# Attention masks placed in PSUM by ScalarE, a sum of squares taken on TensorE, and a new listed order

## The chip, the core and the metric

The kernel runs on one core of a Trainium2 chip. A core has a matrix engine (TensorE, PE in the profile; its weight loads are shown apart as PEld), a vector engine (VectorE, DVE), a scalar engine (ScalarE, ACT), GpSimd (POOL), and SyncE (SP), which here only issues DMAs. Each engine works through its own instructions in the order in which they are written, and waits on semaphores where another engine or a DMA has to be done first. On-chip data lies in SBUF, and the matrix products land in PSUM, which has 8 banks of 512 floats for each of 128 partitions.

The metric is the device time of one launch in microseconds (us). The kernel before was timed three times: 518.71, 516.87 and 521.91 us, median 518.71. The execution whose profile is read below took 516.67 us.

## What is computed

Batched attention with two kinds of masks, then a feed-forward layer with the SoLU activation (h times softmax of h), a layer norm and a second product. Cut to what matters:

```python
# B, H, S, D = 8, 8, 576, 64; d_model 512, d_ff 1024
rel = pos[:, None] - pos[None, :]
mask_local = (rel >= 0) & (rel < 32)                    # heads 0 to 3
mask_strided = (rel >= 0) & (pos_k % 32 == pos_q % 32)  # heads 4 to 7
scores = where(mask, q @ k.T / sqrt(D), -1e9)
x = softmax(scores) @ v              # laid out as 4608 tokens x 512
h = x @ w_in
solu = h * softmax(h)
ln = (solu - mean(solu)) / sqrt(var(solu) + 1e-6) * g_ln
out = ln @ w_out
```

w_in and w_out come as 64-bit floats, and the kernel decodes them on the chip.

## The kernel before

**Tiling.** For each of 8 batches the attention is cut into 5 units, 40 in all; `unit(n)` works on batch n // 5. Units 0 and 1 of a batch are strided (6 and 5 blocks of 54 queries by 54 keys, for two pairs of heads), units 2 to 4 are local (3 blocks of 64 queries by 96 keys). The feed-forward part runs over 36 tiles of 128 tokens, `ff(n)`. A tile can start when the units that write its tokens are done.

**A unit.** `qk` (the step that ends at line 364) fills the two PSUM banks of `s_ps` with the scores of the unit: first four products of a 64x64 unit matrix with the bf16 mask (line 359) write 0 or -8e9 over the banks and open the accumulation, then the products of queries and keys (line 364, four 64x64 quarters of the array side by side) add to them. There is one `s_ps`, so the next unit's `qk` can start only when VectorE has taken the row maximum (L370) and subtracted it into SBUF (L380); for the few units of `BY_BLOCK` ScalarE reads the banks instead (L375). Then come exponentials (L382), row sums (L383), a reciprocal (L387, L388), the scaling on GpSimd (L391), a split into two f16 parts (ScalarE L397, VectorE L398), a transposing DMA into one of two `pt` buffers (SP, L400), the products with the values (`pv`, L421) into `x_ps`, and the split of the result into `xhi` and `xlo` (L439, L440). `pv` of a local unit reads the values partly through a shifted copy `ve`, that of a strided unit through `vd`; SP fills both by DMA from the split values (L335).

**A feed-forward tile.** `g1` does two halves of 12 products into `h_ps` (L482 to L484); maxima, exponentials and sums follow on VectorE and ScalarE (L488 to L498), the norms on GpSimd (L502 to L537), the split into `cc` (L544, L545), a transposing DMA (L548), then two halves of 12 products with w_out (`g2`, L557 to L559) and the store (L565, L566).

**Weights.** `prep_w` loads w_in in four chunks of 1 MB, decodes each (ScalarE L585, VectorE L588 and L589), squares each on ScalarE with a running sum (L598) and has TensorE add the sums over the partitions (L260). A power of two near the root, `w_sc`, then scales the chunks into two f16 parts (L603, L604). `prep_o` does the like for w_out, in four chunks of 1 MB, and folds the mean and the gain into it with eight products (L624). `v_scale(b)` finds such a scale for the values of batch b (ScalarE L299, TensorE L260, VectorE L266 to L272), and takes one column of `s_ps` for its sum; `v_split` splits the values (L320, L321).

**What sets the order.** The steps are recorded with `plan.add(engine, assumed duration, function, reads, writes)`, and then issued in the order of a table of step numbers, `ORDER`, which was found by a search outside the kernel. Each engine, and SP's queue of DMAs, runs its part of that list in order; semaphores guard the data.

Of the kernel before, what the change touches and what calls it, by code (L numbers as in the profile page):

```python
# [20 lines left out]
P = 128  # L21
# [21 lines left out]
SQ = 20  # L43

# [5 lines left out]
EARLY = 4  # L50
BY_BLOCK = (2, 3, 4, 7, 8, 9)
# [22 lines left out]
833 730 857 1074 729 889 704 622 726 890 732 625 731 626-628 613 733 630 734 891 631 705 905 614 737 706 632 878 845 879 735 880 750 906 615 907 835  # L74
# [16 lines left out]
1293 1294 1186-1188 1171 1428 1189 1155 1266 1297 1267 1295 1172 1385 1296 1173 1287 1156 1429 1312 1288 1420 1191 1421 1410 1192 1310 1430 1193 1298  # L91
# [6 lines left out]
1472 1518 1519 1510 1520 1522 1521 1511 1473 1523-1526 1540 1527 1474 1533 1529 1542 1541 1531 1534 1530 1532 1492 1543 1535 1536 1544 1545 1547 1546  # L98
1548 1493 1549-1552 1537 1494 1553 1554 1508 1528 1558 1555 1556 1559 1557 1538 1560 1561 1512 1539 1513 1562 1514 1563 1564
"""  # L100


class Plan:
    def __init__(self):
        self.steps = []
        self.issue = {}
        self.writer, self.readers = {}, {}

# [34 lines left out]
def attn_solu_kernel(ctx: ExitStack, tc: tile.TileContext, qloc, qstr, kloc, kstr, vloc, vstr, w_in, w_out, g, masks, out):  # L143
# [7 lines left out]
    def buf(name, shape, dtype=F32, n=1):  # L151
        return [sb.tile(shape, dtype, name=f"{name}{i}") for i in range(n)]
# [589 lines left out]
```

## Time and profile before

| what | value |
|---|---|
| three timed runs | 518.71, 516.87, 521.91 us |
| the profiled execution | 516.67 us, of which 515.0 us from the first to the last instruction |
| mean granted TensorE clock | 0.983 |
| HBM read, written | 39.24 MB, 9.44 MB |
| `pt` and `cc` transposing DMAs | 40 and 42 issues, median 4.6 and 4.4 us from issue to landing |
| w_in chunks | 4 of 1024 KB, median 14.1 us to landing |

The page gives busy time by engine, the span in 40 slices of 12.9 us, the chain of work that ended last, and the groups of instructions by line, with the mean duration of one and the idle time of the engine before them. A matmul's recorded duration includes the time in the pipeline: successive matmuls start well before the one before has ended, so the cost of a matmul on a full TensorE is read from start to start.

### The profile page before, as it was taken

To read this page: it belongs to the slowest core of one execution; us is meant where nothing else is said; L and a number is where in the kernel's file an instruction comes from. 1 tells how busy PE (TensorE), PEld (TensorE's weight loads), DVE (VectorE), ACT (ScalarE), POOL (GpSimd) and SP (SyncE) were. 2 spreads that over 40 slices of the span, in tenths; PEclk is the share of its full clock that TensorE was granted. 3 is DMA by queue.
4 is the path that set the end of the run, shared out by engine and by line. 5 is a ranking of instruction groups with operands and counts; after the bars stand their busy time and mean duration, and the time that the engine had idled before them with its cause. 6 is when DMAs were issued, how large, how long until landed. Compare 5 with 4: busy or idle time off the path is not lost.

```text
span 515.0 us, 11938 instructions
## 1 busy us (share of the span) xinstructions
PE 469.2 (91%) x4780; PEld 240.6 (47%) x4780; DVE 361.3 (70%) x745; ACT 314.2 (61%) x586; POOL 173.4 (34%) x350
## 2 busy tenths in 40 slices
PE   2223799999999999999999999999999999999997
PEld 2123444445455545454555454544554444444443
DVE  2968898869787777787787757866795577554430
ACT  3897577686755676737665666555564656355541
POOL 5211012635244433323343325035524225115330
PEclk9997599999999999999999999999999999999999
DMA  8999997659879999987999996665996287633542
GB/s 330 376 270 276 297 262 184 189 149 190 171 160 254 207 235 294 234 193 150 216 211 211 246 185 155 103 127 138 233 221 124 62 147 149 134 76 78 123 87 77
DMA packets 155351, 96.90 MB, mean 188 GB/s; under 512 B 138272, under 2 KB 138912, under 8 KB 154784
## 3 DMA queue, kind: packets, MB, share of 16 engines
q1 hardware_dynamic: 150112, 86.71, 76.2%
q10 hardware_dynamic: 5184, 9.44, 5.3%
q8 instruction: 37, 0.61, 0.5%
q14 instruction: 18, 0.15, 0.1%
HBM read 39.24 MB, written 9.44 MB: 95 GB/s over the span
## 4 chain that ended last, share of the span: by engine, by line
PE 79%; DMA 8%; ACT 4%; DVE 4%; SPq 2%; POOL 1%; issue 1%; ACTq 0%; DVEq 0%; POOLq 0%
PE h_ps L482 11%; PE o_ps L557 11%; PE h_ps L484 10%; PE h_ps L483 10%; PE o_ps L559 10%; PE o_ps L558 10%; PE x_ps L421 5%; PE s_ps L364 5%; DMA pt<-p 5%; DMA k<-kloc 2%; PE o_ps L624 2%; PE s_ps L359 1%; DMA vrs<-vstr 1%; ACT raw L492 1%; DVE obuf L640 1%
## 5 line engine op out<-in xcount | busy, mean ns | idle before, releaser
L482 PE MATMUL h_ps<-w,xhi 128*128 128x512 f16 x280 | 106.4, 380 | 1.1 <-DVE raw L494 0.9
L484 PE MATMUL h_ps<-w,xlo 128*128 128x512 f16 x280 | 106.1, 379 | 0.0
L483 PE MATMUL h_ps<-w,xhi 128*128 128x512 f16 x280 | 106.1, 379 | 0.0
L557 PE MATMUL o_ps<-obuf,cc 128*128 128x512 f16 x272 | 103.4, 380 | 0.9 <-issue 0.9
L559 PE MATMUL o_ps<-obuf,cc 128*128 128x512 f16 x272 | 103.1, 379 | 0.0
L558 PE MATMUL o_ps<-obuf,cc 128*128 128x512 f16 x272 | 103.1, 379 | 0.0
L391 POOL TENSOR_TENSOR t<-t,m 128x576 f32<-128x576 f32 (+2 forms) x40 | 48.6, 1218 | 117.6 <-DVE m L388 100.2
L488 DVE TENSOR_REDUCE st<-h_ps 128x1 f32<-128x512 f32 x70 | 46.9, 684 | 53.0 <-PE h_ps L484 52.8
L492 ACT ACTIVATE raw<-h_ps,st,vsc 128x512 f32<-128x512 f32 x62 | 47.9, 775 | 32.0 <-DVE st L490 30.7
L525 POOL TENSOR_SCALAR st<-st 128x1 f32<-128x1 f32 x32 | 12.8, 399 | 152.9 <-DVE st L497 144.3
L498 ACT ACTIVATE raw<-raw,st 128x1024 f32<-128x1024 f32 x36 | 41.3, 1146 | 27.7 <-DVE st L497 21.7
L545 DVE SCALAR_TENSOR_TENSOR cc<-raw,st,cc 128x1024 f16<-128x1024 f32 (+1 forms) x38 | 48.3, 1275 | 12.6 <-ACT cc L544 12.4
L544 ACT ACTIVATE cc<-raw,st 128x1024 f16<-128x1024 f32 (+1 forms) x38 | 41.6, 1100 | 24.8 <-POOL st L534 24.2
L494 DVE SCALAR_TENSOR_TENSOR raw<-h_ps,raw 128x512 f32<-128x512 f32 x70 | 47.4, 682 | 10.3 <-ACT raw L492 9.7
L565 ACT ACTIVATE ob<-o_ps,st 128x512 f32<-128x512 f32 x34 | 23.4, 687 | 48.3 <-PE o_ps L559 38.8
L364 PE MATMUL s_ps<-k,q 64*54 64x54 f32 (+1 forms) x1280 | 41.9, 275 | 4.3 <-DMA k<-kloc 2.6
L370 DVE TENSOR_REDUCE m<-s_ps 128x6 f32<-128x576 f32 (+2 forms) x40 | 30.4, 760 | 21.6 <-PE s_ps L364 21.5
L484 PEld LDWEIGHTS <-xlo 128*128 128x128 f16 x288 | 28.2, 98 | 34.4 <-DVE xlo L440 0.5
L559 PEld LDWEIGHTS <-cc 128*128 128x128 f16 x288 | 28.2, 98 | 34.0
L482 PEld LDWEIGHTS <-xhi 128*128 128x128 f16 x288 | 28.1, 98 | 33.2 <-issue 1.3
L557 PEld LDWEIGHTS <-cc 128*128 128x128 f16 x288 | 28.1, 98 | 33.0 <-issue 1.1
L483 PEld LDWEIGHTS <-xhi 128*128 128x128 f16 x288 | 28.2, 98 | 31.7 <-issue 1.8
(134 smaller groups left out, 760.7 us busy)
## 6 DMA issues: line engine op xcount, KB each, us to landing
out<-ob ACTq DMA_DIRECT2D x36, 256.0 KB, 3.6
vd<-vs SPq DMA_DIRECT2D x16, 384.0 KB, 6.4
q<-qstr SPq DMA_DIRECT2D x8, 594.0 KB, 6.1
k<-kstr SPq DMA_DIRECT2D x8, 594.0 KB, 5.9
q<-qloc SPq DMA_DIRECT2D x8, 576.0 KB, 5.1
k<-kloc SPq DMA_DIRECT2D x8, 576.0 KB, 6.3
raw<-w_in SPq DMA_DIRECT2D x4, 1024.0 KB, 14.1
vrs<-vstr SPq DMA_DIRECT2D x5, 768.0 KB, 7.4
```

Source lines behind the costliest of these rows:

```text
L364: nc.tensor.matmul(s_ps[row : row + nq, pair, i * nk : (i + 1) * nk], q_raw[half][hs, q0 : q0 + (nq - 1) * nqb + 1 : nqb], k_raw[half][hs, ...
L391: add("pool", nx * nk / 520 + 0.03, lambda: nc.gpsimd.tensor_tensor(tv, tv, sm.unsqueeze(2).broadcast_to([P, nx, nk]), op=ALU.mult), r=TM, ...
L482: nc.tensor.matmul(hv[i], xhi[:, cc, tok], whi[:, cc, cols], start=(cc == 0), stop=False)
L483: nc.tensor.matmul(hv[i], xhi[:, cc, tok], wlo[:, cc, cols], start=False, stop=False)
L484: nc.tensor.matmul(hv[i], xlo[:, cc, tok], whi[:, cc, cols], start=False, stop=(cc == 3))
L488: add("dve", 0.69, lambda i=i: nc.vector.tensor_reduce((nm, nm2)[i], hv[i], axis=AX.X, op=ALU.max, negate=True), r=[HH[i]], w=[(ST, "nm", i)])
L492: add("act", 0.73, lambda i=i, q=q: nc.scalar.activation(e[:, parts2[i]], hv[i], AF.Exp, bias=nm, scale=hs, accum_out=q), r=[HH[i], (ST, " ...
L494: add("dve", 0.7, lambda i=i, x=x: nc.vector.scalar_tensor_tensor(u[:, parts2[i]], hv[i], 1.0, e[:, parts2[i]], op0=ALU.mult, op1=ALU.mult ...
L545: add("dve", w / 980 + 0.23, lambda cols=cols: nc.vector.scalar_tensor_tensor(c[:, 1, cols], u[:, cols], r, c[:, 0, cols], op0=ALU.mult, o ...
L557: nc.tensor.matmul(o, ct[:, cc, :], ohi[:, cc, :], start=(cc == 0), stop=False)
L558: nc.tensor.matmul(o, ct[:, cc, :], olo[:, cc, :], start=False, stop=False)
L559: nc.tensor.matmul(o, ct[:, 8 + cc, :], ohi[:, cc, :], start=False, stop=(cc == 7))
```

## The change

Three edits.

1. From unit 6 on (`SEEDED = NU + 1`) the four mask products are gone. A new step on ScalarE, `seed`, copies the bf16 mask into both banks of `s_ps` (f32), once for each unit, and the query-key products add to what it wrote. The step reads the masks and writes `s_ps`, so it waits for the last reader of the unit before, and `qk` waits for it. The assumed duration of `qk` falls by 0.2 us. The column that `v_scale` uses in `s_ps` moves with the batch, and its product no longer opens an accumulation from batch 2 on.
2. In `prep_w` the four squares on ScalarE (L598) are gone. After each chunk's decode, TensorE multiplies the chunk (the upper 16 bits of each float, read as bf16) with itself, in 8 products of 128x128 that all add up in one bank, and after the fourth chunk VectorE takes the diagonal with a running sum (`diag`). The decode scales by a further power of two.
3. `ORDER` is a new table.

```diff
+W_SHIFT = 24
+SEEDED = NU + 1
 ORDER = """
-1 5 8 10 4 11 16 13 12 29 14 9 6 56 155 44 2 57 58 0 71 59 7 15 45 17 60 21 25 72 30 46 61 73 62 47 48 3 50 31 91 74 86 75 76 63 92 77 93 94 87 64 116
+7 3 0 4 8 10 11 16 13 15 12 14 9 29 6 17 25 57 156 21 45 5 58 59 2 1 72 60 61 46 62 73 63 47 74 48 92 75 49 76 51 77 93 78 30 94 52 87 18 31 53 64 95
...
     def pow2_scale(...):
-                nc.tensor.matmul(tot, ones, part.bitcast(BF16)[:, 1:2], start=(i == 0), stop=(i == len(parts) - 1))
+                nc.tensor.matmul(tot, ones, part.bitcast(BF16)[:, 1:2], start=(i == 0 and not adds), stop=(i == len(parts) - 1), skip_group_check=adds)
...
     def v_scale(b):
-        room = (s_ps[:, 1, 511:512], ("s", 1)) if b else (h_ps[2][:, 0:1], ("h", 2))
+        room = (s_ps[:, 1, 512 - b : 513 - b], ("s", 1)) if b else (h_ps[2][:, 0:1], ("h", 2))
...
     def unit(n):
+        mk = (mk_loc[:, 0 if b0 == 0 else 1] if half == 0 else mk_str[:, 0:nb]).rearrange("p x k -> p (x k)")
+        if n >= SEEDED:
+            def seed():
+                nc.scalar.copy(s_ps[:, :, 0 : nb * nk], mk.unsqueeze(1).broadcast_to([P, 2, nb * nk]))
+            add("act", nx * nk / 1200 + 0.17, seed, r=["mask"], w=[("s", 0), ("s", 1)])
         def qk():
-            for pair, h, hs, row in heads:
+            for pair, h, hs, row in heads if n < SEEDED else ():
                 nc.tensor.matmul(s_ps[row : row + D, pair, 0 : nb * nk], unit_sb[hs, hs], mk[hs], start=True, stop=False)
...
-        add("pe", nb * 0.231 + (0.25, 0.09)[half], qk, ...)
+        add("pe", nb * 0.231 + (0.25, 0.09)[half] - (0.2 if n >= SEEDED else 0.0), qk, ...)
...
     def prep_w():
         for cc in range(4):
-            add("act", 1.15, lambda cc=cc: nc.scalar.activation(ob_sb[cc % 2].bitcast(BF16), stage[cc], AF.Square, scale=2.0**-SQ,
-                                                                accum_out=w_sc[:, 4 + cc : 5 + cc]),
-                r=ST[cc], w=[("wm", cc), ("ob", cc % 2)])
-        pow2_scale(w_sc, [w_sc[:, 4 + cc : 5 + cc] for cc in range(4)], ..., (h_ps[0][:, 0:1], ("h", 0)))
+            def gram(cc=cc):
+                x = stage[cc].bitcast(BF16).rearrange("p (f t) -> p f t", t=2)[:, :, 1]
+                for i in range(8):
+                    nc.tensor.matmul(h_ps[0][:, 0:P], x[:, i * P : i * P + P], x[:, i * P : i * P + P], start=(cc == 0 and i == 0), stop=(cc == 3 and i == 7))
+            add("pe", 0.6, gram, r=ST[cc], w=[("h", 0)])
+        add("dve", 0.3, lambda: nc.vector.scalar_tensor_tensor(diag, h_ps[0][:, 0:P], 1.0, unit_sb, op0=ALU.mult, op1=ALU.mult, accum_out=w_sc[:, 4:5]),
+            r=[("h", 0), "unit"], w=["wm"])
+        pow2_scale(w_sc, [w_sc[:, 4:5]], ["wm"], "w_sc", (h_ps[1][:, 0:1], ("h", 1)), mul=2.0**W_SHIFT, shift=0, floor=2.0**-64)
```

Line numbers in the rows of the changed kernel are its own: L411 is the transposing DMA of a unit (L400 before), L339 the copies of values (L335), L285 the loads (L281), L362 the new mask copy, L408 and L450 what L397 and L439 were.

**SP's queue, batch 0, from the transposing DMA of unit 1 to that of unit 2.** `pt1<-p1`, `pt1<-p0` and `pt0<-p2` are the transposing DMAs of units 1, 3 and 2, `ve` the shifted copy of the local values in three pieces, `raw<-w_out` chunks of w_out. Before:

```order
L400 DMA_TRANSPOSE pt1_98<-p1_95 128x10x128
L281 DMA q00_63<-qloc 128x1152
L281 DMA raw0_67<-w_out 128x2x1024
L400 DMA_TRANSPOSE pt1_98<-p0_94 128x12x128
L335 DMA ve0_73<-vl0_71 64x2560
L335 DMA ve0_73<-vl0_71 32x2x1024
L335 DMA ve0_73<-vl0_71 32x2x256
L281 DMA raw0_67<-w_out 128x2x1024
L400 DMA_TRANSPOSE pt0_97<-p2_96 128x12x128
L281 DMA cc0_101<-w_out 128x2x1024
```

Now:

```order
L411 DMA_TRANSPOSE pt1_98<-p1_95 128x10x128
L285 DMA raw0_67<-w_out 128x2x1024
L285 DMA q00_63<-qloc 128x1152
L411 DMA_TRANSPOSE pt1_98<-p0_94 128x12x128
L339 DMA ve0_73<-vl0_71 64x2560
L411 DMA_TRANSPOSE pt0_97<-p2_96 128x12x128
L285 DMA raw0_67<-w_out 128x2x1024
L339 DMA ve0_73<-vl0_71 32x2x1024
L339 DMA ve0_73<-vl0_71 32x2x256
L285 DMA cc0_101<-w_out 128x2x1024
```

Unit 2's transposing DMA moved ahead of the second w_out chunk, and two of the three pieces of `ve` moved behind that chunk.

**ScalarE, batch 0, around the squares of w_in.** `p` rows are the f16 split of a unit, `t,m<-s_ps` its exponentials, `junk,vm1` the squares of the values of batch 1. Before:

```order
L397 CAST p2_96<-t2_87 128x6x96
L299 ACTIVATE junk0_68,vm1_76<-vrs0_70 128x1536
L598 ACTIVATE ob0_102,w_sc0_114<-cc0_101 128x1024
L598 ACTIVATE ob1_103,w_sc0_114<-cc0_101 128x1024
L598 ACTIVATE ob0_102,w_sc0_114<-cc0_101 128x1024
L598 ACTIVATE ob1_103,w_sc0_114<-cc0_101 128x1024
L397 CAST p0_94<-t3_88 128x6x96
L375 ACTIVATE t0_85,m4_93<-s_ps_118,m4_93 128x96 x6
L439 CAST xhi0_99<-x1_ps_123 128x18x18
```

Now:

```order
L303 ACTIVATE junk0_68,vm1_76<-vrs0_70 128x1536
L408 CAST p2_96<-t2_87 128x6x96
L408 CAST p0_94<-t3_88 128x6x96
L386 ACTIVATE t0_85,m4_93<-s_ps_119,m4_93 128x96 x6
L450 CAST xhi0_99<-x1_ps_124 128x18x18
L450 CAST xhi0_99<-x0_ps_123 128x18x18
```

The four squares are gone, and the splits of units 2 and 3 stand next to each other.

**ScalarE, batches 2 and 3, around units 15 and 16.** `raw,st<-h_ps` rows (L492, now L503) are exponentials of feed-forward tiles, `raw<-raw` (L498, now L509) their squares, `cc<-raw` (L544, now L555) their splits, `t<-t` (L382, now L393) the exponentials of a unit. Before:

```order
L439 CAST xhi0_99<-x1_ps_123 128x18x18
L439 CAST xhi0_99<-x0_ps_122 128x18x18
L382 ACTIVATE t2_87<-t2_87 128x576
L397 CAST p0_94<-t0_85 128x6x96
L492 ACTIVATE raw0_67,st3_107<-h2_ps_121,st3_107,vsc1_78 128x512
L492 ACTIVATE raw0_67,st3_107<-h0_ps_119,st3_107,vsc1_78 128x512
```

Now:

```order
L393 ACTIVATE t2_87<-t2_87 128x576
L450 CAST xhi0_99<-x0_ps_123 128x18x18
L362 CAST s_ps_119<-mk_str0_83 128x2x324
L450 CAST xhi0_99<-x1_ps_124 128x18x18
L509 ACTIVATE raw0_67,st2_106<-raw0_67,st2_106 128x1024
L303 ACTIVATE junk0_68,vm0_75<-raw0_67 128x1536
L555 ACTIVATE cc0_101<-raw0_67,st2_106 128x1024
L324 ACTIVATE vs0_72<-vrs0_70,vsc3_80 128x1536
L362 CAST s_ps_119<-mk_str0_83 128x2x270
L503 ACTIVATE raw0_67,st3_107<-h0_ps_120,st3_107,vsc1_78 128x512
```

The mask copy of unit 15 stands between the two copies that empty `x_ps`, and that of unit 16 behind a feed-forward split and a split of the values.

More of the change, by code (lines that the diff above doesn't have):

```diff
@@ L50 @@
 EARLY = 4
+SEEDED = NU + 1
 BY_BLOCK = (2, 3, 4, 7, 8, 9)
 ORDER = """
[19 rows of a table removed]
-833 730 857 1074 729 889 704 622 726 890 732 625 731 626-628 613 733 630 734 891 631 705 905 614 737 706 632 878 845 879 735 880 750 906 615 907 835
[16 rows of a table removed]
-1293 1294 1186-1188 1171 1428 1189 1155 1266 1297 1267 1295 1172 1385 1296 1173 1287 1156 1429 1312 1288 1420 1191 1421 1410 1192 1310 1430 1193 1298
[6 rows of a table removed]
-1472 1518 1519 1510 1520 1522 1521 1511 1473 1523-1526 1540 1527 1474 1533 1529 1542 1541 1531 1534 1530 1532 1492 1543 1535 1536 1544 1545 1547 1546
-1548 1493 1549-1552 1537 1494 1553 1554 1508 1528 1558 1555 1556 1559 1557 1538 1560 1561 1512 1539 1513 1562 1514 1563 1564
[7 rows of a table added]
+238 214 345 239 230 240 242 311 231 241 329 243 256 330 215 309 244 331 245 346 334 468 368 335 255 246 336 257-259 232 248 260 123 261 249 347 233
[20 rows of a table added]
+959 1247 843 1248 1249 1046 1269 1298 984 1297 1270 844 1044 985 971-975 1003 986 1271 987 1272 1058 1112 1283 1273 960 1113 1094 988 1114 1061 989
[10 rows of a table added]
+1200 1345 1422 1348 1420 1334 1346 1434 1360 1423 1201 1478 1457 1466 1479 1446 1421 1362 1335 1361 1336 1480 1219 1481 1363 1364 1445 1349-1351 1444
+1435 1367 1482 1220 1436 1368 1365 1352 1483 1366 1353 1380 1333 1221 1354 1438 1355 1382 1484 1356 1369 1439 1467 1337 1381 1468 1383 1371 1469 1384
+1385 1470 1458 1370 1386 1471 1338 1459 1372 1387 1460 1437 1492 1339 1374 1375 1490 1376 1357 1491 1388 1485 1389 1493 1390 1391 1494 1472 1495 1392
+1358 1496 1510 1359 1473 1394 1512 1497 1498 1511 1499-1501 1377 1513 1514 1474 1502 1515 1395 1517 1393 1486 1373 1396 1378 1487 1504 1488 1516 1518
+1532 1379 1530 1533 1519 1505 1520 1521 1506 1522 1397 1531 1534 1535 1524 1398 1537 1538 1536 1539 1525 1541 1552 1399 1540 1526 1523 1503 1542 1550
+1553 1544 1507 1551 1554 1557 1555 1558 1556 1508 1559 1545 1560-1562 1575 1509 1568 1564 1565 1577 1567 1566 1527 1578 1569 1576 1571 1570 1579 1582
+1546 1528 1580 1583 1581 1584 1586 1572 1529 1585 1587 1573 1588 1589 1563 1543 1593 1590 1591 1547 1594 1592 1595 1596 1548 1597 1549 1574 1598 1599
 """
@@ L204, in attn_solu_kernel @@
     (w_sc,) = buf("w_sc", [P, 8])
+    (diag,) = buf("diag", [P, P], BF16)
     (o_sc,) = buf("o_sc", [P, 16])
@@ L249, in attn_solu_kernel, with pow2_scale @@
     add("dve", 0.05, lambda: nc.vector.memset(k_raw[0][:, 0:KPAD], 0.0), w=[("k", 0)])
-    def pow2_scale(dst, parts, r, w, room, top=14, mul=1.0, square=None):
+    def pow2_scale(dst, parts, r, w, room, top=14, mul=1.0, square=None, adds=False, shift=SQ, floor=2.0**-40):
         tot, T = room
@@ L268, in fn @@
         def fn():
-            nc.vector.tensor_scalar(dst[:, 0:1], dst[:, 0:1], 2.0 ** (64 + SQ - top), 2.0**-40, op0=ALU.mult, op1=ALU.max)
+            nc.vector.tensor_scalar(dst[:, 0:1], dst[:, 0:1], 2.0 ** (64 + shift - top), floor, op0=ALU.mult, op1=ALU.max)
             nc.vector.reciprocal(dst[:, 1:2], dst[:, 0:1])
@@ L300, in v_scale @@
             add("act", (1.36, 1.58)[a], square, r=[("vr", a, raw)], w=["junk", ("vm", b % 2, a)])
-        room = (s_ps[:, 1, 511:512], ("s", 1)) if b else (h_ps[2][:, 0:1], ("h", 2))
-        pow2_scale(sc, [vm[:, 0:1], vm[:, 1:2]], [("vm", b % 2, a) for a in range(2)], ("vsc", b % 4), room, 8, 1.0 / P_SCALE)
+        room = (s_ps[:, 1, 512 - b : 513 - b], ("s", 1)) if b else (h_ps[2][:, 0:1], ("h", 2))
+        pow2_scale(sc, [vm[:, 0:1], vm[:, 1:2]], [("vm", b % 2, a) for a in range(2)], ("vsc", b % 4), room, 8, 1.0 / P_SCALE, adds=b > 1)
         def hscale():
@@ L352, in unit @@
         t4 = tv.rearrange("p (c x) k -> p c x k", c=2)
+        mk = (mk_loc[:, 0 if b0 == 0 else 1] if half == 0 else mk_str[:, 0:nb]).rearrange("p x k -> p (x k)")
[3 more added lines that the diff above has]
+            add("act", nx * nk / 1200 + 0.17, seed, r=["mask"], w=[("s", 0), ("s", 1)])
         def qk():
-            mk = (mk_loc[:, 0 if b0 == 0 else 1] if half == 0 else mk_str[:, 0:nb]).rearrange("p x k -> p (x k)")
             heads = [(pair, h, slice(h * D, h * D + D), (h ^ pair) * D) for pair in range(2) for h in range(2)]
-            for pair, h, hs, row in heads:
+            for pair, h, hs, row in heads if n < SEEDED else ():
                 nc.tensor.matmul(s_ps[row : row + D, pair, 0 : nb * nk], unit_sb[hs, hs], mk[hs], start=True, stop=False)
@@ L364, in qk @@
                     nc.tensor.matmul(s_ps[row : row + nq, pair, i * nk : (i + 1) * nk], q_raw[half][hs, q0 : q0 + (nq - 1) * nqb + 1 : nqb],
-                                     k_raw[half][hs, k0 : k0 + nk], start=False, stop=(i == nb - 1))
-        add("pe", nb * 0.231 + (0.25, 0.09)[half], qk, r=[("q", half), ("k", half), "mask", "unit"], w=[("s", 0), ("s", 1)])
+                                     k_raw[half][hs, k0 : k0 + nk], start=False, stop=(i == nb - 1), skip_group_check=n >= SEEDED)
+        add("pe", nb * 0.231 + (0.25, 0.09)[half] - (0.2 if n >= SEEDED else 0.0), qk, r=[("q", half), ("k", half), "mask", "unit"], w=[("s", 0), ("s", 1)])
         SS = [("s", 0), ("s", 1)]
@@ L574, in attn_solu_kernel, with decode @@
     LAST_ROOM = (cc_sb[:, 3:5].bitcast(I32), [*CT[1], *CT[2]])
-    def decode(dst, src, n, w, room):
+    def decode(dst, src, n, w, room, shift=0):
         room, RAW = room
@@ L582, in decode @@
         load(2.61, room, src, RAW, [("pt", 1)] if n == 4 else [])
-        add("act", 1.14, lambda: nc.scalar.activation(dst, w1.bitcast(F32), AF.Prelu, scale=2.0**-112, alpha=-(2.0**32)), r=RAW, w=w)
+        add("act", 1.14, lambda: nc.scalar.activation(dst, w1.bitcast(F32), AF.Prelu, scale=2.0 ** (-112 - shift // 8), alpha=-(2.0**32)), r=RAW, w=w)
         def bits():
@@ L596, in prep_w @@
         for cc in range(4):
-            decode(stage[cc], w_in[cc * P : (cc + 1) * P, :].rearrange("p (a f) -> p a f", a=2), cc, ST[cc], ROOMS[cc])
-            add("act", 1.15, lambda cc=cc: nc.scalar.activation(ob_sb[cc % 2].bitcast(BF16), stage[cc], AF.Square, scale=2.0**-SQ,
-                                                                accum_out=w_sc[:, 4 + cc : 5 + cc]),
-                r=ST[cc], w=[("wm", cc), ("ob", cc % 2)])
-        pow2_scale(w_sc, [w_sc[:, 4 + cc : 5 + cc] for cc in range(4)], [("wm", cc) for cc in range(4)], "w_sc", (h_ps[0][:, 0:1], ("h", 0)))
+            decode(stage[cc], w_in[cc * P : (cc + 1) * P, :].rearrange("p (a f) -> p a f", a=2), cc, ST[cc], ROOMS[cc], W_SHIFT)
+            def gram(cc=cc):
[6 more added lines that the diff above has]
+        pow2_scale(w_sc, [w_sc[:, 4:5]], ["wm"], "w_sc", (h_ps[1][:, 0:1], ("h", 1)), mul=2.0**W_SHIFT, shift=0, floor=2.0**-64)
         for cc in range(4):
```

76 rows, old and new, of the table ORDER are left out of this document.

## The prediction

> **What bounds the kernel now.** I read the page first: shares, slices, chain. Each digit of the slices is a tenth of 12.9 us.
>
> ```profile
> PE 469.2 (91%) x4780; PEld 240.6 (47%) x4780; DVE 361.3 (70%) x745; ACT 314.2 (61%) x586; POOL 173.4 (34%) x350
> PE   2223799999999999999999999999999999999997
> ACT  3897577686755676737665666555564656355541
> PEclk9997599999999999999999999999999999999999
> PE 79%; DMA 8%; ACT 4%; DVE 4%; SPq 2%; POOL 1%; issue 1%; ACTq 0%; DVEq 0%; POOLq 0%
> ```
>
> From the fifth slice to the end TensorE has hardly a gap; in the first four it works two to three tenths of the time. So there are two stages: a start, and a long stretch in which only less TensorE work, or fewer waits of TensorE, change the time. Next the chain in order of time, for the start, and the busy time by stretches (columns: PE, PEld, DVE, ACT, POOL, clock, DMA share, GB/s).
>
> ```profile
> 23.93 6.29 DMA vrs<-vstr
> 31.02 9.78 DMA pt<-p
> 40.84 1.12 PE x_ps L421 x40
> 41.98 2.35 SPq L400
> 44.38 0.59 SPq L335
> 47.05 0.60 SPq L281
> 47.70 7.78 DMA pt<-p
> 55.52 1.17 PE x_ps L421 x36
> 56.70 5.42 PE o_ps L624 x6
> ...
> 20.00:30.00 10.00, 1.58 (x29) 1.33 (x29) 9.69 (x13) 8.77 (x27) 1.15 (x1) 1.00 1.08 310
> 30.00:40.00 10.00, 4.51 (x113) 3.88 (x113) 5.18 (x19) 9.11 (x27) 2.02 (x2) 1.00 1.10 252
> 50.00:60.00 10.00, 5.65 (x76) 3.59 (x76) 8.27 (x12) 4.10 (x9) 0.65 (x1) 0.50 1.09 333
> ```
>
> The DMA engines are full (shares of 1.08 to 1.10) and the chain runs over landings: unit 1's transposing DMA lands at 40.80, its `pv` frees the buffer for unit 3's, and behind that SP issues the pieces of `ve`, a chunk of w_out and unit 2's transposing DMA, which lands at 55.48. From 55.52 on TensorE is the bound.
>
> **The mask products on TensorE.** The timeline of a unit between two feed-forward halves (start, duration, engine, line):
>
> ```profile
> 197.63 0.38 PE L558 MATMUL o_ps<-obuf,cc 128*128 128x512 f16 x1
> 197.84 0.38 PE L559 MATMUL o_ps<-obuf,cc 128*128 128x512 f16 x1
> 198.15 0.32 PE L359 MATMUL s_ps<-mk_loc,unit 64*64 64x288 bf16 x4
> 198.30 0.84 PE L364 MATMUL s_ps<-k,q 64*64 64x96 f32 x24
> 199.07 0.39 PE L482 MATMUL h_ps<-w,xhi 128*128 128x512 f16 x1
> ...
> 16.59 1.25 PE L364 MATMUL s_ps<-k,q 64*64 64x96 f32 x24 [2.58 <-DMA k<-kloc]
> 21.45 1.22 PE L364 MATMUL s_ps<-k,q 64*64 64x96 f32 x24
> ```
>
> Four mask products run side by side in the four quarters of the array, and cost 198.30 - 198.15 = 0.15 us, not four times 0.32. The step from a 128-row product to a quarter one (197.84 to 198.15, 0.31, where two products stand 0.21 apart) stays: the query-key products are quarter ones too. What may come back is the first f32 weight load, which ran under the masks. Unit 2 shows it: its query-key products began after a wait for a DMA, without masks just ahead, and took 1.25 us; those of unit 3, behind masks, 1.22. So 0.03 comes back and 0.12 a unit is saved. The ends are 0.15 and nothing (the whole 0.15 covered weight loads, which is the third rival).
>
> The Trainium skill (TensorE: Matmul & The Clock Gate, Part 3, what overlaps and what doesn't) says that a weight load runs ahead of products in flight only where their row groups differ, and a 128-row product holds all of them. By it the first f32 loads would be bare and the saving near nothing, 4 us less than in my sum; unit 2's row speaks against it, and I go by the row.
>
> Units 6 to 39 lose their masks. Unit 6 lies in the start, where TensorE waits anyway; the other 33 save 33 x 0.12 = 4.0 us (0 to 5.0).
>
> **The mask copies on ScalarE.** In no row of before does ScalarE write PSUM. The nearest is a cast of as many elements between SBUF tiles:
>
> ```profile
> L397 ACT CAST p<-t 128x576 f16<-128x576 f32 x24 | 16.0, 667 | 2.5 <-POOL t L391 2.0 <-ACT ob L565 0.5
> ...
> 158.54 0.83 DVE L380 TENSOR_TENSOR t<-s_ps,m 128x648 f32<-128x648 f32 x1
> 160.23 0.31 PE L359 MATMUL s_ps<-mk_str,unit 64*64 64x270 bf16 x4
> ...
> ACT raw L492 <- DVE st L490: 42.7, 23, 5.6
> ACT cc L544 <- POOL st L534: 24.2, 18, 3.1
> 209.00 0.39 PE L557 MATMUL o_ps<-obuf,cc 128*128 128x512 f16 x1 [0.94 <-issue]
> ```
>
> 34 copies of 0.67 us are 23 us on an engine with 39% idle; by themselves they cost nothing. What matters is the chain through `s_ps`: VectorE's subtraction, then the copy, then the products. Before, unit 16's masks began at 160.23, 0.86 us after the subtraction of unit 15 had ended (158.54 + 0.83); TensorE was busy with a feed-forward half in between. That is about the tightest place: in the old list six units stand one half behind the unit before, in the new one seven (11, 12, 13, 17, 21, 32, 36). A copy of 0.67 with a hand-over on each side just fits into 0.86 if ScalarE is free; if it is in the middle of an instruction, TensorE waits, and with it the feed-forward halves queued behind. I take 0.2 us for each of the seven, 1.4 us; the ends are 0 and, for each, a wait like ScalarE's own two above (66.9 us in 41, 1.6 each), 11 us. Behind a copy that waits on ScalarE stand the exponentials of the unit before and of feed-forward tiles; their readers, VectorE and GpSimd, have slack outside such a place (70% and 34% busy).
>
> Of the few waits of TensorE in the long stretch, the largest is the 0.94 at 209. A new order may remove these or add others; I see no reason for either sign and put nothing in the sum.
>
> **The sum of squares.**
>
> ```profile
> L598 ACT ACTIVATE ob<-cc 128x1024 bf16<-128x1024 f32 x4 | 4.2, 1041 | 0.0
> 31.79 1.04 ACT L598 ACTIVATE ob<-cc 128x1024 bf16<-128x1024 f32 x1
> 34.90 1.04 ACT L598 ACTIVATE ob<-cc 128x1024 bf16<-128x1024 f32 x1
> L421 PE MATMUL x_ps<-pt,vl 96*64 96x64 f16 x384 | 15.0, 201 | 6.0 <-DVE xlo L440 5.9
> L440 DVE TENSOR_TENSOR xlo<-x_ps,xhi 128x270 f16<-128x270 f32 x16 | 6.8, 430 | 1.8 <-ACT xhi L439 1.8
> ```
>
> ScalarE loses four squares, 4.2 us, between 31.8 and 36. TensorE gains 32 products of 128 columns; from 0.21 us for 512 columns I estimate 0.05 each, 0.1 at half the clock, 1.7 to 3.4 us, in a window where it was busy 1.6 of 10 us, so they are hidden. VectorE gains one pass over 128 columns, under 0.43 (the 270-column row), and was idle half of 30 to 40. The scale is ready sooner, but not by 4 us: in the new order its last products stand behind the sum for batch 1's values, whose load landed at 30.22 in the chain. And what follows the scale waits for landings anyway: up to unit 1's transposing DMA both lists issue the same loads and copies in another order, the DMA engines are full, and it should land near 40.8 again. So I take nothing here; the ends are 0 and -4.2.
>
> **The start behind that landing.**
>
> ```profile
> 51.81 0.37 PE L421 MATMUL x_ps<-pt,vl 96*64 96x64 f16 x6 [5.95 <-DVE xlo L440]
> 52.58 0.40 PE L421 MATMUL x_ps<-pt,vl 96*64 96x64 f16 x6
> 54.05 1.19 ACT L585 ACTIVATE obuf<-raw 128x1024 f32<-128x1024 f32 x1 [3.09 <-DMA raw<-w_out]
> 66.59 0.38 PE L482 MATMUL h_ps<-w,xhi 128*128 128x512 f16 x1
> ```
>
> SP now issues unit 2's transposing DMA before the w_out chunk and two pieces of `ve` behind it. Unit 3's `pv` needs one of these, and stands ahead of unit 2's on TensorE. Before, the chunk was there at 54.05, and unit 2's transposing DMA behind it at 55.48. The same bytes are now to land in another order, so the last piece lands near 55.5, and unit 3's `pv`, which ran from 51.81 to 52.98 while TensorE waited, now opens the long stretch: +1.1 us (0 to 1.2). The w_out chunk, and the decode and products (L624) that wait for it, come about as before. The masks of unit 7 that fall away there are in the 33.
>
> **The sum.** -4.0 (masks) + 1.4 (waits for copies) + 0 (squares) + 1.1 (start) = -1.5 us. The profiled execution took 516.67 (515.0 and 1.67 around it), so 515.2 for one like it. The median of the three runs lies 2.0 above that execution; against it the forecast is 518.71 - 1.5 = 517.2, 0.3% less.
>
> **Rivals.**
> - *The start shortens.* If the chain ahead of 40.8 hangs on ScalarE rather than on the DMA engines, the 4.2 us of squares come off, and unit 3's 1.1 with them: 518.7 - 4.0 + 1.4 - 4.2 = 511.9. For it: ScalarE is busy 9.1 of 10 us there and its wait for batch 1's load is in the chain. Against it: DMA shares over 1 from 20 to 40. It is faster by over 1% once the start gains 2.6 us.
> - *TensorE waits on ScalarE.* ScalarE takes its list in order, and a mask copy that stands behind an exponential (L492) or a split (L544) waits as long as these do: 42.7 us in 23 waits and 24.2 in 18, near 1.6 each. Where the list puts a copy right behind one, TensorE sits through the rest of the wait. If 6 of the 33 units lose 1.6 us, and the others 0.1 (2.7), that is 12.3 in place of 1.4: 528.1. It decides for slower by over 1% from 8.1 us of waits, 0.25 a unit. For it: the copies of units 15 and 16 stand behind work that hangs on TensorE and VectorE. Against it: ScalarE already stands in TensorE's way in the same manner, with the copies that empty `x_ps` and the stores that empty `o_ps`, and the slices show TensorE at 9 throughout.
> - *The masks hid the loads.* The first four weight loads take the place of the masks' 0.15: no gain on TensorE, and 517.2 + 4.0 = 521.2. Unit 2's 1.25 against 1.22 speaks against it.
>
> **Chances and range.** Forecast 0.55, start 0.22, ScalarE 0.13, loads 0.10. A difference within 1% can't be told from none in a measurement of this kernel. Faster by over 1% (under 513.5): the 0.22 and 0.03 of the forecast (no waits at all, the whole 0.15 saved), 0.25. Slower (over 523.9): 0.13 and 0.02 of the third, 0.15. Within: 0.60. The range runs from 511.0, just below the start's rival, to 523.0, above the third; the forecast's own is 513.7 (masks 5.0, no other loss) to 521 (waits of 0.75 in each tight place).
>
> **What would show it.** Query-key groups from unit 6 on that start 0.31 after a feed-forward product, with the next one 0.12 us sooner than before, show the first step; 0.15 more between them shows the loads. An idle row of TensorE ahead of L364's successor, ended by ScalarE's copy, shows the waits, and their sum against 1.4 sizes them; one over 1 us is the second rival. A landing of unit 1's transposing DMA well before 40.8, or the first feed-forward product well before 66.6, shows the start's rival. Long new waits of TensorE for VectorE or DMAs in the stretch from 70 to 500 would make the forecast wrong by the order alone.

## The result, and the profile after

The changed kernel took 522.40 us (median of 20 runs, 519.65 to 527.66), the kernel before 516.23 in the runs beside it (20 runs, 513.64 to 521.91). The ratio is 1.0125, with a 95% interval of 1.0101 to 1.0148: slower by 1.25%, where 0.3% faster was forecast. The profiled execution took 523.59 us, 521.9 of them span, against 515.0 before: 6.9 more.

The page of the changed kernel, busy time and TensorE's slices (13.0 us each):

```profile
PE 471.6 (90%) x4673; PEld 242.6 (46%) x4673; DVE 360.6 (69%) x748; ACT 330.1 (63%) x612; POOL 181.7 (35%) x350
PE   2244579999989999999999999999999999999996
```

The trace has 107 products fewer, and yet TensorE is busy longer. The fifth slice is a 5 in place of a 7, the sixth a 7 in place of a 9. The timeline of TensorE (and SP's row for unit 3's transposing DMA) shows where the start went:

```profile
41.91 1.06 PE L432 MATMUL x_ps<-pt,vd 118*64 118x54 f16 x32
45.05 0.42 PE L432 MATMUL x_ps<-pt,vd 118*64 118x54 f16 x8 [2.08 <-issue]
45.51 2.43 SPq L411 DMA_TRANSPOSE pt<-p  x1
...
58.01 0.37 PE L432 MATMUL x_ps<-pt,ve 96*64 96x64 f16 x6 [7.94 <-DMA ve<-vl]
...
70.48 0.37 PE L432 MATMUL x_ps<-pt,ve 96*64 96x64 f16 x6 [3.13 <-DMA pt<-p]
...
71.58 2.08 PE L642 MATMUL o_ps<-obuf,gmat 128*128 128x512 f32 x2
73.45 0.55 PE L493 MATMUL h_ps<-w,xhi 128*128 128x512 f16 x1
```

The same stretch before (TensorE, and SP's row for unit 4's transposing DMA):

```profile
40.84 1.10 PE L421 MATMUL x_ps<-pt,vd 118*64 118x54 f16 x40
...
57.00 3.60 SPq L400 DMA_TRANSPOSE pt<-p  x1
...
64.94 0.28 PE L421 MATMUL x_ps<-pt,ve 96*64 96x64 f16 x6
...
65.63 1.12 PE L624 MATMUL o_ps<-obuf,gmat 128*128 128x512 f32 x2
```

The first feed-forward product comes at 73.45, 6.86 after the 66.59 of before: the whole difference of the spans. Unit 1's value products, 40 in one go before, stop after 32 for 2.08 us in which the profile shows nothing to wait for ("issue"). The chain of waits names the rest:

```profile
41.98 0.99 PE x_ps L432 x32
42.97 2.59 issue x2
...
51.12 6.24 DMA raw<-w_out
...
57.39 1.17 ACT obuf L596
...
58.58 1.24 DVE obuf L600
...
60.31 10.12 DMA pt<-p
...
70.48 1.17 PE x_ps L432 x19
71.65 2.01 PE o_ps L642 x2
```

Three pieces make the 6.86. Unit 4's transposing DMA is issued at 60.31 in place of 57.00 (+3.3). It lands 10.1 us later in place of 7.9 (+2.2). From its landing to the first feed-forward product it takes 3.0 in place of 1.7 (+1.3): TensorE had stood idle for 3.13 us, and its two products behind the wait (L642) took 2.08 together, where the two ahead of the first feed-forward product took 1.12 before, so it ran at about half speed (the granted clock of these microseconds is shown further down).

From the first feed-forward product to the end it is 448.4 us, as before (448.4). So the long stretch gained nothing in sum. A unit in it, and TensorE's waits from 75 us on (engine, line, releaser: total, times, longest), first after, then before:

```profile
202.85 0.38 PE L570 MATMUL o_ps<-obuf,cc 128*128 128x512 f16 x1
203.16 0.95 PE L375 MATMUL s_ps<-k,q 64*64 64x96 f32 x24
204.04 0.39 PE L568 MATMUL o_ps<-obuf,cc 128*128 128x512 f16 x1
```

```profile
PE o_ps L568 <- DMA cc<-cc: 1.6, 1, 1.6
PE h_ps L493 <- DVE raw L505: 1.2, 2, 0.9
PE s_ps L568 <- ACT ob L576: 0.8, 1, 0.8
PE s_ps L375 <- ACT s_ps L362: 0.5, 1, 0.5
```

```profile
PE o_ps L557 <- issue: 0.9, 1, 0.9
PE h_ps L482 <- DVE raw L494: 0.9, 1, 0.9
PE s_ps L260 <- ACT junk L299: 0.7, 1, 0.7
PE h_ps L482 <- ACT xhi L439: 0.2, 1, 0.2
```

Between two feed-forward halves a local unit now takes 204.04 - 202.85 = 1.19 us, before 199.07 - 197.84 = 1.23. Over all local units that stand so, the medians are 1.192 (14 units) and 1.223 (13): 0.03 saved, not 0.12. With slightly more for the strided units (0.03 to 0.04) that is 1.1 us in 33 units, and the waits, 4.1 against 2.7, take it back.

### The profile page after: what moved, and what is told of

It reads as the page before. It is cut to its first block, busy times and chain, and to the rows that moved or that the text cites. A ratio compares the mean times of both kernels' runs of the same rounds, so it can differ in the third digit from the quotient of the medians.

```text
span 521.9 us, 11769 instructions
## 1 busy us (share of the span) xinstructions
PE 471.6 (90%) x4673; PEld 242.6 (46%) x4673; DVE 360.6 (69%) x748; ACT 330.1 (63%) x612; POOL 181.7 (35%) x350
## 4 chain that ended last, share of the span: by engine, by line
PE 79%; DMA 8%; DVE 4%; ACT 4%; issue 2%; SPq 1%; POOL 1%; ACTq 0%; DVEq 0%; POOLq 0%
PE o_ps L568 11%; PE h_ps L493 11%; PE o_ps L569 11%; PE o_ps L570 11%; PE h_ps L495 10%; PE h_ps L494 10%; PE s_ps L375 7%; PE x_ps L432 5%; DMA vrs<-vstr 4%; DMA pt<-p 2%; DMA cc<-cc 2%; DMA raw<-w_out 1%; PE o_ps L642 1%; PE s_ps L568 1%; PE s_ps L570 1%
## 5 line engine op out<-in xcount | busy, mean ns | idle before, releaser
L402 POOL TENSOR_TENSOR t<-t,m 128x576 f32<-128x576 f32 (+2 forms) x40 | 47.4, 1186 | 115.6 <-DVE m L399 87.4
L536 POOL TENSOR_SCALAR st<-st 128x1 f32<-128x1 f32 x32 | 16.1, 503 | 144.7 <-DVE st L508 144.3
L503 ACT ACTIVATE raw<-h_ps,st,vsc 128x512 f32<-128x512 f32 x62 | 47.8, 773 | 20.0 <-DVE st L501 19.0
L555 ACT ACTIVATE cc<-raw,st 128x1024 f16<-128x1024 f32 (+1 forms) x38 | 41.7, 1102 | 23.5 <-POOL st L545 16.7
L509 ACT ACTIVATE raw<-raw,st 128x1024 f32<-128x1024 f32 x36 | 41.2, 1145 | 19.6 <-DVE st L508 17.7
L375 PE MATMUL s_ps<-k,q 64*54 64x54 f32 (+1 forms) x1280 | 45.5, 286 | 3.7 <-DMA k<-kstr 2.2
L375 PEld LDWEIGHTS s_ps<-k,q 64*54 64x54 f32 (+1 forms) x1280 | 39.8, 201 | 16.7 <-issue 9.7
L494 PEld LDWEIGHTS <-xhi 128*128 128x128 f16 x288 | 28.2, 98 | 33.1 <-issue 2.8
```

Source lines behind the costliest of these rows:

```text
L375: nc.tensor.matmul(s_ps[row : row + nq, pair, i * nk : (i + 1) * nk], q_raw[half][hs, q0 : q0 + (nq - 1) * nqb + 1 : nqb], k_raw[half][hs, ...
L402: add("pool", nx * nk / 520 + 0.03, lambda: nc.gpsimd.tensor_tensor(tv, tv, sm.unsqueeze(2).broadcast_to([P, nx, nk]), op=ALU.mult), r=TM, ...
L494: nc.tensor.matmul(hv[i], xhi[:, cc, tok], wlo[:, cc, cols], start=False, stop=False)
L503: add("act", 0.73, lambda i=i, q=q: nc.scalar.activation(e[:, parts2[i]], hv[i], AF.Exp, bias=nm, scale=hs, accum_out=q), r=[HH[i], (ST, " ...
```

## The experiments

Each ratio below is to runs of the kernel before on the same chip, with its 95% interval. The changed kernel came out at 1.0125 and, once more, at 1.0108 (1.0072 to 1.0144).

### What the masks cost

**The masks alone, old order.** The first edit in the kernel before; each mask copy stands in ScalarE's old list ahead of the first step that began after the scores were free.

```diff
-            for pair, h, hs, row in heads:
+            for pair, h, hs, row in heads if n < SEEDED else ():
...
+            add("act", nx * nk / 1200 + 0.17, seed, r=["mask"], w=[("s", 0), ("s", 1)])
```

> The kernel before with the first edit alone: masks from ScalarE from unit 6 on, each copy put into ScalarE's old list where the scores of the unit before are free. Squares and the order of all other steps as before. Loads theory (the masks had hidden the first float32 weight loads): a local unit between two feed-forward halves takes 1.19 us in place of 1.22, 33 units save about 1.1 us, and with a few waits for ScalarE the time lies within 2 us of the kernel before. Rival, the prediction's own price: 0.12 saved per unit, the group at 1.10, the time about 4 us below the kernel before. The first feed-forward product at 66.6 by both.

Measured: ratio 1.0007 (0.9975 to 1.0039), span 514.6. The first feed-forward product came at 67.14, and from there to the end it took 447.5, 0.9 less than before; the whole time does not show that 0.9. A local unit took 1.19 (199.54 - 198.35):

```profile
198.35 0.38 PE L570 MATMUL o_ps<-obuf,cc 128*128 128x512 f16 x1
198.66 0.95 PE L375 MATMUL s_ps<-k,q 64*64 64x96 f32 x24
199.54 0.39 PE L493 MATMUL h_ps<-w,xhi 128*128 128x512 f16 x1
```

The unit has the price of the loads theory, and there is no slowdown: the loss of the changed kernel isn't this edit's.

**Masks behind the scores.** In the kernel before, for the local units; the scores of these units come out changed by it, and only the time is read.

```diff
-                    ..., start=False, stop=(i == nb - 1))
+                    ..., start=(not half), stop=bool(half) and i == nb - 1, skip_group_check=True)
+            if not half:
+                put(False, True)
```

> The kernel before with the four mask products of the 24 local units put behind the products of queries and keys in place of ahead of them; the strided units and the order of all steps as before. Loads theory (placed ahead, the masks run while the first float32 weights load): a local unit between two feed-forward halves takes about 0.1 us more, 1.33 in place of 1.22, the step from the first to the fifth product of queries and keys grows from 0.08 to 0.19, and the 20 local units of the long stretch add about 2 us. Rival (the masks cost their 0.15 and hide nothing): 1.22 as before and no difference.

Timeline of a unit:

```profile
198.59 0.38 PE L565 MATMUL o_ps<-obuf,cc 128*128 128x512 f16 x1
198.90 0.95 PE L368 MATMUL s_ps<-k,q 64*64 64x96 f32 x24
199.67 0.31 PE L360 MATMUL s_ps<-mk_loc,unit 64*64 64x288 bf16 x4
199.91 0.39 PE L488 MATMUL h_ps<-w,xhi 128*128 128x512 f16 x1
```

199.91 - 198.59 = 1.32, 0.09 more than with the masks ahead. The first product of queries and keys stands 0.19 ahead of the fifth, as it does without masks; where the masks stand ahead, it is 0.08. So the masks had hidden 0.11 us of weight loads, against their own 0.15. The whole time does not show the 1.8 us of 20 such units (ratio 1.0005, 0.9968 to 1.0042); the unit's rows do.

### The pause in unit 1's value products

**Products for the sum of squares alone, old order.**

```diff
-            add("act", 1.15, ... AF.Square ..., r=ST[cc], w=[("wm", cc), ("ob", cc % 2)])
+            add("pe", 0.6, gram, r=ST[cc], w=[("h", 0)])
```

> The kernel before with the second edit alone: 32 products of w_in's chunks with themselves in the places of the four squares, all else in the old order. Code theory: TensorE's instruction stream pauses at the same count of products and weight loads as before (about the 349th product), which the 32 extra products move into unit 1's value products; these pause there for about 2 us, unit 3's transposing DMA is issued near 44 in place of 41.98, and the first feed-forward product comes 1.5 to 3 us later than 66.6. Rival, the pause in the changed kernel comes from its order of DMAs: no pause inside unit 1's value products here, the first feed-forward product at 66.6 or up to 1 us earlier.

Timeline (TensorE, and SP's row):

```profile
39.72 0.78 PE L431 MATMUL x_ps<-pt,vd 118*64 118x54 f16 x32 [0.15 <-DVE xlo L450]
43.00 0.31 PE L431 MATMUL x_ps<-pt,vd 118*64 118x54 f16 x8 [2.50 <-issue]
...
43.34 1.44 SPq L410 DMA_TRANSPOSE pt<-p  x1
```

The pause is there, in the old order of DMAs, after the same 32 products. But the first feed-forward product came at 66.61 and the ratio is 1.0032 (0.9993 to 1.0072): a miss on the second half of the expectation. Unit 1's transposing DMA had landed at 39.00 in this execution, 1.8 sooner than before, which makes up for most of the pause; that the rest of the list had slack for what was left is inferred.

**Half of the products, changed kernel.** The sum is taken over half of the columns and doubled.

```diff
-                for i in range(8):
+                for i in range(0, 8, 2):
...
-        ... diag, h_ps[0][:, 0:P], 1.0, unit_sb ...
+        ... diag, h_ps[0][:, 0:P], 2.0, unit_sb ...
```

> The changed kernel with four of the eight products of each chunk with itself (the sum of squares is taken over half of the columns and doubled): 16 products and 16 weight loads fewer ahead of unit 1's value products. Code theory: the pause of 2.08 us at 42.97 leaves unit 1's value products and falls into unit 6's scores, which wait for other work anyway; unit 3's transposing DMA is issued near 43.4 in place of 45.51 and the first feed-forward product comes about 2 us earlier than 73.45. Rival (the pause is a moment of crowded DMA, whatever TensorE runs): a pause between 43 and 45 as before, and no gain.

```profile
42.51 0.86 PE L432 MATMUL x_ps<-pt,vd 118*64 118x54 f16 x40
...
43.40 1.61 SPq L411 DMA_TRANSPOSE pt<-p  x1
...
45.12 1.62 PE L375 MATMUL s_ps<-k,q 64*54 64x54 f32 x40 [1.75 <-ACT s_ps L362]
```

All 40 products run in one go, though they start 0.6 later than in the changed kernel, and unit 3's transposing DMA is issued 2.1 sooner. The ratio is 0.9998 (0.9966 to 1.0030): sixteen products fewer take the whole loss away. It is not their own time that does it, since unit 1's value products start no sooner. What is left of the pause is 0.11 us among unit 6's scores. The first feed-forward product comes at 68.85, 4.6 sooner, where 2 were expected: unit 4's transposing DMA flies (from issue to landing) 7.6 us in place of 10.1.

**The changed kernel once more.** No edit.

> The changed kernel once more, to see which parts of its start repeat from one execution to the next. The pause of TensorE behind its 349th product should repeat within 0.5 us of 2.08, unit 3's transposing DMA within 1 us of 45.5. If the long flight of unit 4's transposing DMA (10.1 us from issue to landing) belongs to the order, it repeats and the first feed-forward product lies within 1 us of 73.45; if it was that execution's, the product comes 2 to 3 us earlier.

```profile
42.91 1.06 PE L432 MATMUL x_ps<-pt,vd 118*64 118x54 f16 x32
45.94 0.42 PE L432 MATMUL x_ps<-pt,vd 118*64 118x54 f16 x8 [1.96 <-issue]
```

```profile
61.46 10.88 DMA pt<-p
```

Pause (timeline) and flight (chain) both repeat; the first feed-forward product came at 75.35, 1.9 later than in the first execution, where 1 was expected at most.

### SP's queue

**The pieces of ve first, as before.**

```diff
 L411 DMA_TRANSPOSE pt<-p (unit 3)
 L339 DMA ve<-vl 64x2560
-L411 DMA_TRANSPOSE pt<-p (unit 2)
-L285 DMA raw<-w_out
 L339 DMA ve<-vl 32x2x1024
 L339 DMA ve<-vl 32x2x256
+L285 DMA raw<-w_out
+L411 DMA_TRANSPOSE pt<-p (unit 2)
```

> The changed kernel, with SP's queue behind unit 3's transposing DMA as it was before: the three pieces of ve, then the w_out chunk, then unit 2's transposing DMA. Queue theory (the pieces of ve behind the chunk cost the start): unit 3's value products run some 6 us earlier, near 52, in the wait ahead of unit 2's, the first feed-forward product comes 3 us or more earlier than 73.45. Rival (the whole start is late since unit 3's transposing DMA is issued 3.5 us late, and the same bytes have to land in either order): unit 2's transposing DMA lands near 59, unit 4's near 70, and the first feed-forward product comes at most 1.2 us earlier.

Measured: ratio 1.0032 (1.0008 to 1.0057), first feed-forward product at 69.85, 3.6 sooner. The landing of unit 2's transposing DMA, 59.04, is the rival's; the gain is the first theory's. Unit 3's value products were done at 54.0, behind the last piece of ve (53.06), and unit 4's transposing DMA, issued at 60.53 as late as ever, landed at 66.96. The pause was there (1.80 us).

**Unit 4's transposing DMA ahead of the last w_out chunk.** Two rows of SP's queue exchanged.

> The changed kernel with unit 4's transposing DMA ahead of the last w_out chunk in SP's queue. In the changed kernel it was issued at 60.31, 0.48 us behind that chunk, and landed at 70.44, the chunk at 67.37. Chunk theory (the DMA is late since it shares the engines with a chunk issued just ahead): it lands 2.5 us or more earlier, near 67, and the first feed-forward product comes 2.5 us earlier than 73.45. Rival (it is late by its own issue, behind unit 2's value products): it lands within 1 us of 70, and nothing is gained.

Timeline of SP, chain and waits:

```profile
60.33 1.32 SPq L411 DMA_TRANSPOSE pt<-p  x1
61.76 0.97 SPq L285 DMA_DIRECT2D raw<-w_out  x1
```

```profile
61.76 8.20 DMA raw<-w_out
```

```profile
PE h_ps L264 <- DVE o_sc L647: 1.9, 1, 1.9
```

It landed at 64.21, 3.9 us after its issue in place of 10.1, and the first feed-forward product came at 69.35, 4.1 sooner. But the ratio is 1.0073 (1.0042 to 1.0104): the chunk now lands at 69.96, its decoding follows it in the chain, and TensorE waits from 73.6 to 75.6 for the scale of w_out. About half of the gain, 2.0 of 4.1 us, is lost again behind the first feed-forward product.

### Is there more to be had?

**Three repairs of the start**: half of the products, ve ahead of unit 2's transposing DMA, unit 4's ahead of the last chunk.

> The changed kernel with three repairs of its start together: four of eight products of each w_in chunk with itself, the three pieces of ve ahead of unit 2's transposing DMA and the w_out chunk, unit 4's transposing DMA ahead of the last w_out chunk. If the start is lost by the pause for code and by landings in a bad order: unit 3's transposing DMA at 43.4, unit 2's value products near 54, unit 4's transposing DMA issued near 55, the first feed-forward product near 66, and a time 1 to 3 us below the kernel before. Rival (behind 55 the start is bound by VectorE and the decoding of w_out whatever lands when): the first feed-forward product at 68 or later and a time not below the kernel before.

Ratio 1.0025 (0.9995 to 1.0056), first feed-forward product at 67.86: near the rival's 68, and no gain. Unit 2's value products ended at 54.8 and TensorE then waited 3.9 us for the decoding of w_out.

**Half of the products, and unit 4's transposing DMA ahead.**

> The changed kernel with four of eight products a chunk, and unit 4's transposing DMA ahead of the last w_out chunk. If the flight of that DMA still costs something behind the removed pause (7.6 us with the half products, 3.9 where it went ahead), the first feed-forward product comes 2 us earlier than 68.85 and the time falls 1 to 2 us below that of the half products alone. Rival (the last w_out chunk, now behind it, becomes late, as it did where the DMA was moved alone): the first feed-forward product is earlier, but TensorE waits for the scale of w_out 5 to 8 us later, and the time stays within 1 us of the half products alone.

Ratio 1.0038 (1.0015 to 1.0061). The first feed-forward product came 3.4 sooner (65.45), and TensorE waited 2.0 for w_out's scale behind it, as the rival has it; but the time is some 2 us above that of the half products alone (0.9998), where the rival allowed 1.

**Both edits in the old order, half of the products.**

> Both edits in the order of the kernel before: the masks from ScalarE as in the first experiment, and products of w_in's chunks in the places of the squares, but only four of eight a chunk. Code theory: the 16 extra products move the 698th row of TensorE's program to the first products of unit 6's scores, which wait for VectorE anyway, so no pause falls on unit 1's value products; these end near 40.7, unit 3's transposing DMA is issued near 41 in place of 41.98, and with 1.1 us for the masks the time lies 1.5 to 3 us below the kernel before (ratio 0.994 to 0.997). Rival (the start is bound by VectorE and by landings of w_out, so what comes sooner is lost again): the first feed-forward product at 66 or later, and the masks' 1 us alone, ratio 0.998.

Ratio 1.0020 (0.9991 to 1.0049). No pause in unit 1's value products, but these began at 41.10, not at 39.7 as in the run of the products alone: unit 1's transposing DMA had landed at 40.57. Unit 3's was issued at 42.14, where 41 was expected. First feed-forward product 66.74: the rival's, though the masks' 1 us that it allowed does not show in the time.

**The second edit alone, old order, half of the products.**

> The second edit alone in the order of the kernel before, with four of eight products a chunk, masks on TensorE throughout. Code theory: no pause in unit 1's value products, which end near 40.7; unit 3's transposing DMA is issued near 41, 2 us sooner than with all products in that order (43.34), and the first feed-forward product comes 1 us or more sooner than 66.6. Rival (the start is bound elsewhere): the DMA sooner, the first feed-forward product still at 66 to 67, the time that of the kernel before.

Ratio 0.9986 (0.9955 to 1.0016), no pause there either; unit 1's transposing DMA landed at 41.91 and unit 3's was issued at 43.27: no sooner than with the pause. The first feed-forward product came at 68.62, later than either theory had it; this execution took 518.94, 3.2 above the median of its runs. The 39.00 of the first run of this edit was that execution's; over these kernels that landing lies between 39.0 and 41.9.

**Half of the products and the old order of ve, changed kernel.**

> The changed kernel with four of eight products a chunk, and SP's queue behind unit 3's transposing DMA as it was before (ve, then the w_out chunk, then unit 2's transposing DMA): the two repairs that each brought the time back to within 0.4% of the kernel before, now together. If their gains add: unit 3's transposing DMA at 43, unit 2's landing near 56.5, the first feed-forward product near 66.5, and, with the masks' 1.1 us, a time 1 to 2 us below the kernel before. Rival (each removes the same lateness of unit 4's transposing DMA, and VectorE and w_out bound the rest): the first feed-forward product at 67.5 or later, the time within 0.3% of the kernel before.

The chain, from unit 3's transposing DMA on:

```profile
44.04 1.45 SPq L411
...
49.22 9.05 DMA pt<-p
...
59.48 4.86 PE o_ps L642 x8
```

Unit 2's transposing DMA flies 9.05 us and opens TensorE's work at 58.3. Ratio 1.0008 (0.9979 to 1.0037), first feed-forward product at 67.86: the two gains do not add. No version here beats the kernel before by what can be measured. With half of the products both edits cost nothing that can be measured, in either order, and most or all of the loss of 1.25% can be taken away in more than one place.

## Why the prediction was wrong, step by step

The sign was wrong. That 522.40 still lies inside the stated range is luck: its upper end was drawn above the third rival, and the time came near it by the start, for which the sum had 1.1 us and 1.2 at most. The prediction also held that a difference within 1% can't be told from none; with 20 runs of each kernel the interval was 0.24% to each side.

**Masks, -4.0: measured -1.1.** The step that failed is "so 0.03 comes back and 0.12 a unit is saved". It is the other way round: 0.12 comes back and 0.03 is saved, near the third rival. Unit 2's row, from which the 0.03 was read, lies in the start, where the fours of products follow each other at 0.16 us; in the long stretch they follow at 0.11. And the length of a row hides part of the load: from its first product to its fifth, unit 2 took 0.22 us and unit 3, behind masks, 0.16. The Trainium skill (TensorE: Matmul & The Clock Gate, Part 3, what overlaps and what doesn't) had spoken against the row: by it a weight load runs ahead of products in flight only where their row groups differ. For the quarter loads the trace agrees: the first starts 0.31 us behind the last 128-row product (203.16 - 202.85), not under it. For the 128-row loads of a feed-forward half it does not: the load for the product at 202.85 starts at 202.64, under the product before.

**Waits for ScalarE's copies, +1.4: measured +0.5** in the long stretch, one wait ahead of unit 8. The copies took 0.60 to 0.72, as taken from the cast. The second rival (TensorE waits on ScalarE) did not come.

**The order of the long stretch, 0: measured +0.9**, waits for a feed-forward tile's transposing DMA (1.6), for VectorE (1.2) and for a store (0.8), less the 2.7 of before. The 1.6 is not the order's alone: with the same order it was 1.0 in the second execution and absent with half of the products. With the masks and the copies that is the 0.0 of the long stretch, within 0.3.

**Squares, 0.** Unit 1's transposing DMA landed at 40.52, near 40.8 as forecast, so the first rival (the start shortens) did not come. But the 32 products were priced by their own time alone. What they cost is their place in TensorE's program: its 698th row of products and weight loads, behind which it pauses in these kernels, had been among unit 6's scores (0.24 us there before) and now fell on unit 1's value products, which SP's queue waits for. The half-products runs show that the loss begins here. It takes the new order with it: in the old order the same pause cost nothing that can be measured (1.0032, 0.9993 to 1.0072).

**The start, +1.1: measured +6.9.** The step that failed is "the w_out chunk, and the decode and products (L624) that wait for it, come about as before". All stood behind unit 3's transposing DMA, issued at 45.51 in place of 41.98: 2.1 by the pause, 1.1 since unit 1's value products began later, behind unit 5's scores (which waited for ScalarE's exponentials until 40.29), the rest in between. What I had taken as fixed, that DMA's start, was what moved. The second w_out chunk landed at 57.36, where it was 54.03 before, and its decoding frees the buffer of the last chunk, which stands ahead of unit 4's transposing DMA in the queue: that is the 3.3. The last piece of ve landed at 58.09, where 55.5 was forecast, and 2.2 of flight and 1.3 of half speed came on top. The undoing of the order that I had priced gave 3.6 of the 6.9 back with the pause still there, so the parts overlap: each repair takes away the same long flight.

**Still open** is why that flight is 10.1 and 10.9 us in the changed kernel and 3.9 to 8.5 elsewhere. Windows of the changed kernel (columns as in the prediction) show the DMA engines busy (shares of 0.85 and more) while little is moved, 115 GB/s in the second row:

```profile
62.00:66.00 4.00, 4.00 (x27) 1.73 (x29) 3.86 (x8) 1.94 (x4) 0.20 (x1) 1.00 1.37 278
66.00:70.00 4.00, 1.35 (x14) 0.42 (x8) 2.72 (x4) 2.39 (x5) 0.90 (x1) 1.00 0.85 115
70.00:74.00 4.00, 3.52 (x40) 1.94 (x41) 1.12 (x1) 2.52 (x6) 0.00 (x0) 0.57 1.06 208
```

The chunk just ahead seems to have a part in it (exchanged, the flight is 3.9, and 4.2 with half of the products). But with that chunk 0.5 us ahead it also flew 6.4, with ve first and with both edits in the old order; and with the three repairs, where it was issued 3.9 us ahead of the chunk, it flew 7.5. The third row's clock, 0.57, is the half speed behind the wait.

## What to carry to other kernels

An instruction added to an engine has a place in its program besides its duration: where a pause stands behind the same count in several kernels, look at what the added instructions push onto it, and whether a queue waits for that. A duration read in a stage at a low pace does not price the same work in a stage at full pace. A slip of 2 us in the release of a buffer that a DMA queue waits for can cost more than twice as much (here 2.1 us sooner gave 4.6 back), since everything behind it in the queue lands elsewhere.

## What the runs showed of the hardware

TensorE paused behind its 698th row (349 products and as many loads) in seven of the fourteen profiles. It was 1.8 to 2.5 us where the rows just ahead were short (32 value products in 0.8 to 1.1 us), and 0.24, 0.11 or none where it had waited 1.3 us or more for something else 8 to 21 products ahead. In the trace's packet records a packet of 16 KB on the queue marked "instruction" began to move 2.3 to 2.7 us ahead of the end of each of the seven pauses (for example before 42.61 to 44.98, after 42.35 to 45.05, the products alone in the old order 40.65 to 43.00). In the seven profiles without a pause, too, the 350th product began 2.3 to 2.8 us behind the start of such a packet, never sooner. That the pause is the loading of code is inferred from this and from its fixed count; the bytes themselves were not varied. The Trainium skill (Runtime: NRT & Kernel Launch, Instruction fetch mechanics) says that programs come in blocks of 16 KiB and that the crossing is mostly hidden. If the pause is such a crossing, up to 2.5 us of it was not hidden here.
